# Attention and soft MoE on one core: output tiles of strided tokens, a first head pair loaded ahead, and zero matmuls moved

## The chip, the core and the metric

The kernel runs on one core of one Trainium2 chip. TensorE (PE) multiplies, VectorE (DVE) and ScalarE (ACT) work on tiles, GpSimd (POOL) does a little of that and issues the loads, SyncE (SP) issues the stores. The metric is the device time of one execution in microseconds (us). The kernel before took 154.47 us, the median of three executions (153.16, 154.95 and 154.47).

## What is computed

There are 4 batches, 8 heads, 768 tokens and 64 values per head. Some heads (retrieval heads) see all earlier tokens, the others the first 4 tokens and a window of 64. The attention output of all heads, 3072 tokens of 512 values, is the input x of a soft mixture of 8 experts with 4 slots each.

```python
scores = np.where(mask, q @ k.T / 8, -1e9)      # per batch and head
x = softmax(scores) @ v                          # -> (3072, 512)
logits = x @ phi                                 # phi (512, 32)
d = softmax over tokens of logits                # columns
slot_input = d.T @ x                             # 32 slots
slot_out[e] = np.maximum(slot_input[e] @ w1[e], 0) @ w2[e]
c = softmax over slots of logits                 # rows
out = c @ slot_out                               # (3072, 512) fp32
```

w1 is (8, 512, 1024) and w2 (8, 1024, 512), in fp32.

## The kernel before, in words

The order of all work is written out by hand in one table, ORDER (line 20): Plan.run (line 108) emits one operation after the other, so each engine gets its instructions in that order, and waits for data where it needs them. Names in the table are an operation, a batch or pair, and a part; /A, /D and /P put it on ACT, DVE or POOL.

Loads. All big inputs go through POOL's queue and are cast from fp32 to bf16 on the way. L{q,k,v}{b} (load_qkv, line 250) loads one batch of q, k or v as 96 partitions of 2 x 2048 values, 768 KB written. Partition 24n + t holds token block t of head pair n, so rows 0 to 23 belong to pair 0 (heads 0 and 4). Lw0 to Lw7 are w1 of the eight experts, Lw8 to Lw15 their w2 (load_w, line 263), 1024 KB written each. Twelve buffers (slot) serve raw q, k, v and the weights; Lw12 to Lw15 (lines 656 to 660) go into memory that the attention has freed: parts of qk, vx, xv, and qk again.

Attention. For every batch, T/E (transposes, line 374) transpose the raw rows on PE, 16 transposes and one copy a part, four parts for each of q, k and v. For each of 16 pairs p (4 per batch), QK.p.g makes five groups of scores, EX.p.g their exponentials on ACT, MK.p.g the masks on DVE; V2/VB transpose v, PV.p.i multiplies, NM.p normalises, XT/XE transpose the result into xT.

Experts. For each batch LG makes the logits, EL their exponentials (tile eT, slots along the partitions, tokens along the row), DS and SA sum x over the tokens for each slot. After the last batch SI forms slot_input, H.e.c is the first expert layer (four experts at a time), HR its ReLU, TH/HE a transpose, and W2.e multiplies expert e of 8 into the tile pv; W2.7 is split into a left and a right half. SO.0 and SO.1 scale the halves into slot_out.

Output. EE.b (emit_ee, line 640) copies the exponentials of batch b into expT, so that out_lhs (line 716) is 128 neighbouring columns: an output tile gi (six of them, r = 0 to 3) then holds tokens 512 gi + 4 p + r on partition p. RW (line 721) sums each token's exponentials, OMf multiplies exponentials and slot_out, OEf scales by the inverse sum on ACT or DVE, and STf (line 800) stores: ten stores of 128 partitions, of 1, 2 or 4 rows r each. The stores are SP's only long work, and SP issues them in order.

Zero matmuls. fill (line 324) multiplies tiles of zeros and keeps PE busy. Z0 and Z60 to Z67 stand in the first half, Z1 to Z4 between the steps after the last pair, and Z5 (line 734), eight of them, between W2.6 and W2.7, which is made to wait for it.

Of the kernel before, what the change touches and what calls it, by code (L numbers as in the profile page):

```python
# [20 lines left out]
Lri zero warm Lq0 tables ident Lk0 keypos Tq0.3 flags Tq0.1 Z0 hm0 Eq0.1/A Tq0.2 Eq0.3/D Eq0.2/A Tq0.0 slottab  # L21
Z62 Tk0.3 Eq0.0/D Ek0.3/D ones Tk0.0 Lv0 Z60 Tk0.2 Ek0.0/D Tk0.1 Z61 Ek0.1/D Ek0.2/A QK.0.1 Tv0.1 hm3 Lw0 Lq1
Ev0.1/D EX.0.1 QK.0.0 Tv0.0 EX.0.0 QK.0.3 Ev0.0/D Lk1 EX.0.3 Tv0.2 MK.0.1 Tv0.3 Z66 hm1 Ev0.2/D QK.0.2 Ev0.3/A
Z64 MK.0.3 MK.0.0 V2.0 EX.0.2 QX.0 VB.0/A Z63 V2.3 hm2 QK.0.4 V2.1 VF.0/D VB.3/D MK.0.2 EXX.0 PV.0.0 QK.1.1
EX.0.4 V2.2 Lphi0 PV.0.1 PV.0.2 VB.2/D QK.1.0 PV.0.3 Lv1 EX.1.1 VB.1/D Lw1 Tq1.1 MK.1.1 QK.1.3 EX.1.0 MK.0.4
# [5 lines left out]
MK.3.1 QK.4.4 MK.3.2 Ev1.1/A Lv2 EX.4.4 QK.4.2 Tv1.2 Ev1.2/D MK.3.4 Tv1.0 EX.4.2 PV.3.0 PV.3.1 QK.4.0 Lw3
Tv1.3 PV.3.2 Ev1.0/D QK.4.1 Ev1.3/D PV.3.3 EX.4.0 PV.3.4 V2.4 MK.4.0 Lw4 EX.4.1 QK.4.3 VB.4/D PV.3.5 V2.6
QK.5.0 XT.2 Lw5 EX.4.3 Z65 NM.3 VB.6/A XT.3 XE.2/D EX.5.0 MK.4.1 MK.4.3 XE.3/A QK.5.3 Lq3 Tq2.1 QK.5.1 VF.4/P
MK.5.0 PV.4.0 Eq2.1/D Tq2.0 PV.4.1 EX.5.3 Tq2.2 QX.1 MK.4.2 phi PV.4.2 EX.5.1 EXX.1 PV.4.3 Eq2.2/A MK.5.1
MK.4.4 LG.0 Eq2.0/D QK.5.4 MK.5.3 Tk2.2 Ek2.2/D EL.0 V2.5 EX.5.4 PV.4.4 VB.5/D QK.5.2 TE.0 PV.4.5 Lk3 EX.5.2
MK.5.4 EG.0/D VF.5/P QK.6.0 Tk2.0 NM.4 Ek2.0/D QK.6.1 EX.6.0 MK.5.2 DS.0 QK.6.4 VF.6/P PV.5.0 EX.6.1 PV.5.1
V2.7 SA.0 PV.5.2 QK.6.2 EX.6.4 MK.6.0 PV.5.3 Tv2.1 QK.6.3 PV.5.4 PV.5.5 EX.6.2 MK.6.1 VB.7/D Ev2.1/D XT.4
QK.7.1 Lv3 EX.6.3 MK.6.4 XE.4/A Tk2.1 MK.6.2 QK.7.4 NM.5 MK.6.3 EX.7.1 Tk2.3 PV.6.0 Ek2.1/D PV.6.1 Ek2.3/D
PV.6.2 EX.7.4 QK.7.2 Tq2.3 PV.6.3 QK.7.0 Lw6 EX.7.2 MK.7.1 Eq2.3/D PV.6.4 MK.7.2 PV.6.5 EX.7.0 QK.7.3 Tv2.0
QK.8.2 EX.7.3 NM.6 Ev2.0/D EX.8.2 VF.7/P Tv2.2 Lw7 MK.7.0 QK.8.0 Tv2.3 PV.7.0 PV.7.1 QK.8.1 EX.8.0 Ev2.2/D  # L40
EX.8.1 XT.6 PV.7.2 QX.2 EXX.2 MK.7.3 Ev2.3/D V2.11 XE.6/D MK.7.4 PV.7.3 MK.8.1 VB.11/D QK.8.3 MK.8.2 V2.8
PV.7.4 QK.8.4 PV.7.5 V2.10 EX.8.3 VB.8/D MK.8.0 NM.7 EX.8.4 XT.5 QK.9.1 VF.8/P VB.10/A QK.9.3 EX.9.1 PV.8.0
PV.8.1 PV.8.2 XT.7 XE.5/D MK.8.3 MK.8.4 V2.9 QK.9.2 XE.7/D PV.8.3 PV.8.4 EX.9.3 VB.9/D QK.9.0 PV.8.5 Tq3.0
MK.9.3 VF.10/P MK.9.1 Tq3.2 EX.9.2 QK.10.2 NM.8 EX.9.0 VF.9/P Eq3.2/D LG.1 Tq3.1 EX.10.2 EL.1 Lw8 QK.9.4
Eq3.0/D MK.9.0 Tk3.2 Eq3.1/D MK.9.2 QK.10.0 PV.9.0 EX.9.4 EX.10.0 TE.1 MK.10.2 EG.1/D PV.9.1 PV.9.2 QK.10.1
Tk3.0 MK.9.4 PV.9.3 Ek3.2/D QK.10.3 Ek3.0/D EX.10.1 PV.9.4 PV.9.5 QK.10.4 EX.10.3 MK.10.0 Tk3.3 NM.9 EX.10.4
QK.11.2 Ek3.3/D DS.1 EX.11.2 PV.10.0 QK.11.0 MK.10.1 Tk3.1 PV.10.1 SA.1 EX.11.0 QK.11.1 Tq3.3 VF.11/P Ek3.1/D
# [794 lines left out]
```

## Time and profile before

| | |
|---|---|
| median of three executions | 154.47 us |
| the profiled execution | 154.55 us |
| its span, first to last instruction | 152.7 us |
| mean TensorE clock granted | 0.969 |
| PE, DVE, ACT, POOL busy | 87%, 74%, 70%, 22% of the span |
| bytes read from and written to HBM | 52.50 MB, 6.29 MB |
| loads on POOL's queue | 26.22 MB written, 83.8% of sixteen DMA engines' span |

A span is counted from the first to the last instruction in the profile; the time of the execution holds some 1.8 us more. In the lists of instructions PE is the matmuls and PEld the weight loads; the operand names are the program's tiles, written <- read. An idle time in brackets is that of the engine just before the instruction, with what ended it.

### The profile page before, as it was taken

How to read it: one execution, taken by the hardware profiler on the slowest of the kernel's cores; microseconds unless marked ns; L12 is line 12 of the kernel's file. 1: busy time of each engine (PE TensorE's matmuls, PEld its weight loads, DVE VectorE, ACT ScalarE, POOL GpSimd, SP SyncE). 2: the span in 40 equal slices, each digit the busy share in tenths (PEclk: the TensorE clock that was granted, in tenths of full speed). 3: DMA queues.
4: the chain of work that ended last, by engine and by line, in shares of the span. 5: the costliest groups of instructions: out<-in, count | busy, mean ns of one | idle time of the engine just before them, and what ended most of it. 6: DMA issues, size and time to landing. Idle time of an engine off the chain costs nothing.

```text
span 152.7 us, 5227 instructions
## 1 busy us (share of the span) xinstructions
PE 133.0 (87%) x2313; PEld 83.1 (54%) x2313; DVE 113.4 (74%) x257; ACT 107.5 (70%) x124; POOL 33.5 (22%) x51
## 2 busy tenths in 40 slices
PE   6999799999999999999989999998999689787100
PEld 2355456676677657677656676665673348232000
DVE  3955698999978799999998998999975322166900
ACT  3023699999999999999879999999917710266300
POOL 6910005750031060505520202405110000000000
PEclk9999999999999999999999999999999959999975
DMA  2999999999999999999999999999999992059995
GB/s 34 200 215 224 213 211 211 217 219 225 201 215 213 227 210 212 225 203 216 211 229 215 212 212 223 210 215 219 219 212 215 221 204 58 4 178 411 417 423 219
DMA packets 6950, 32.91 MB, mean 215 GB/s; under 512 B 1296, under 2 KB 1296, under 8 KB 4496
## 3 DMA queue, kind: packets, MB, share of 16 engines
q0 software_dynamic: 4800, 26.22, 83.8%
q1 hardware_dynamic: 2128, 6.37, 10.7%
q8 instruction: 18, 0.29, 0.7%
q14 instruction: 4, 0.03, 0.1%
HBM read 52.50 MB, written 6.29 MB: 385 GB/s over the span
## 4 chain that ended last, share of the span: by engine, by line
PE 59%; DVE 17%; DMA 8%; ACT 5%; issue 3%; POOL 2%; DVEq 0%; POOLq 0%; ACTq 0%
PE pv L522 13%; PE sc L406 13%; PE tr L387 9%; DMA slot<-in_v_dram 8%; DVE pt L418 5%; DVE slot L774 4%; PE sc L330 4%; PE tr L547 4%; PE tr L438 3%; DVE xv L535 3%; PE pv L742 3%; PE sc L561 3%; PE sc L687 3%; ACT pt L474 2%; DVE qk L234 2%
## 5 line engine op out<-in xcount | busy, mean ns | idle before, releaser
L474 ACT ACTIVATE pt<-sc 128x1024 bf16<-128x1024 f32 x80 | 77.6, 1026 | 4.8 <-PE sc L406 3.4
L418 DVE TENSOR_TENSOR pt<-pt,msk 128x512 bf16<-128x512 bf16 (+1 forms) x80 | 37.8, 503 | 1.2 <-ACT pt L474 1.2
L406 PE MATMUL sc<-qk 64*128 64x512 bf16 (+3 forms) x256 | 32.5, 309 | 0.0
L522 PEld LDWEIGHTS <-pt 128*128 128x128 bf16 x640 | 24.7, 97 | 9.1 <-issue 6.4
L522 PE MATMUL pv<-vx,pt 128*128 128x65 bf16 x352 | 27.9, 193 | 0.9 <-DVE xv L535 0.7
L387 PE MATMUL tr<-ident,slot 96*64 96x96 bf16 x768 | 24.1, 209 | 1.7 <-DMA slot<-in_v_dram 0.9
L454 POOL TENSOR_TENSOR vf<-vx,fm 128x528 bf16<-128x528 bf16 x14 | 15.5, 1112 | 44.8 <-DVE vx L234 43.0
L387 PEld LDWEIGHTS <-slot 96*64 96x64 bf16 x768 | 18.9, 110 | 10.6 <-issue 7.7
L522 PE MATMUL pv<-vf,pt 128*128 128x65 bf16 x288 | 22.7, 195 | 0.0
L330 PE MATMUL sc<-zero 128*128 128x512 bf16 x66 | 19.5, 429 | 1.2 <-DVE zero L321 1.2
L234 DVE COPY qk<-tr 128x768 bf16<-128x768 bf16 x28 | 14.9, 550 | 4.7 <-PE tr L387 4.5
L535 DVE TENSOR_TENSOR xv<-pv,rs 128x768 bf16<-128x768 f32 x16 | 15.3, 958 | 0.6
L406 PEld LDWEIGHTS <-qk 64*128 64x128 bf16 x256 | 9.2, 94 | 7.2 <-issue 1.6
L234 DVE COPY xT<-tr 128x768 bf16<-128x768 bf16 (+1 forms) x15 | 8.6, 570 | 5.2 <-PE tr L708 4.2
L239 POOL DMA_DIRECT2D slot<-in_moe_w_dram x12 | 6.8, 569 | 22.7 <-PE tr L387 16.3
L330 PEld LDWEIGHTS <-zero 128*128 128x128 bf16 x66 | 6.2, 108 | 9.1 <-issue 4.4
L232 ACT COPY qk<-tr 128x768 bf16<-128x768 bf16 x4 | 3.2, 797 | 10.8 <-PE tr L387 10.8
L234 DVE COPY xv<-tr 128x768 bf16<-128x768 bf16 x14 | 7.6, 552 | 1.9 <-PE tr L387 1.7
L547 PE MATMUL tr<-ident,xv 128*128 128x128 bf16 x96 | 8.1, 220 | 0.0
L438 PE MATMUL tr<-ident,xv 128*128 128x128 bf16 x96 | 8.0, 220 | 0.0
L234 DVE COPY vx<-tr 128x768 bf16<-128x768 bf16 x12 | 6.4, 551 | 1.0 <-PE tr L438 1.0
L547 PEld LDWEIGHTS <-xv 128*128 128x128 bf16 x96 | 5.6, 97 | 2.1 <-issue 1.8
(102 smaller groups left out, 135.3 us busy)
## 6 DMA issues: line engine op xcount, KB each, us to landing
slot<-in_moe_w_dram POOLq DMA_DIRECT2D x12, 1024.0 KB, 25.5
slot<-in_q_dram POOLq DMA_DIRECT2D x4, 768.0 KB, 18.4
slot<-in_k_dram POOLq DMA_DIRECT2D x4, 768.0 KB, 21.4
slot<-in_v_dram POOLq DMA_DIRECT2D x4, 768.0 KB, 23.7
out_dram<-slot SPq DMA_DIRECT2D x3, 1024.0 KB, 5.6
out_dram<-slot SPq DMA_DIRECT2D x5, 512.0 KB, 3.6
qk<-in_moe_w_dram POOLq DMA_DIRECT2D x2, 1024.0 KB, 18.3
vx<-in_moe_w_dram POOLq DMA_DIRECT2D x1, 1024.0 KB, 21.5
```

The lines of the kernel that those rows point to most:

```text
L234: nc.vector.tensor_copy(dst, src)
L239: emit=lambda o: e.dma_start(dst(), src))
L330: nc.tensor.matmul(scb[buf.slot][:, 0, :], zero[:, 0:128], zero, start=True, stop=True)
L387: nc.tensor.transpose(t[64 * i:64 * (i + 1), :, s, :], rv[:, i, 8 * c + s, :], ident[0:96, 0:96])
L406: nc.tensor.matmul(scb[sc.slot][:, i, c:c + 128 * nb], kk, qq.rearrange("p b c -> p (b c)"), start=True, stop=True)
L418: e.tensor_tensor(pT[:, :, 0:w], pT[:, :, 0:w], mh[:, :, c:c + w], op=ALU.mult)
L438: nc.tensor.transpose(t[:, 128 * j:128 * (j + 1)], vT[:, 6 * n + j, :], ident)
L454: e.tensor_tensor(vfs[VFb[p].slot], vv, mm, op=ALU.mult)
L474: nc.scalar.activation(pTs[PTb[b, n].slot][:, :, 512 * g:512 * (g + 1)], scb[sc.slot], ACT.Exp, scale=scale)
L522: nc.tensor.matmul(pvb[:, h, 65 * i:65 * (i + 1)], lt, rhs, start=(j == 0), stop=(j == i))
L535: nc.vector.tensor_tensor(xo, pvw[:, :, :, 0:64], r.rearrange("p i (j o) -> p i j o", o=1).to_broadcast([P, 2, 6, 64]), op=ALU.mult)
L547: nc.tensor.transpose(t[:, 128 * i:128 * (i + 1)], xv[:, i, 128 * n:128 * (n + 1)], ident)
```

## The change

- Output tiles of strided tokens. EE and expT go. The stationary operand is read straight from eT, in which a token stands 16 columns from the next one used (ef). Tile gi = 0 to 3 holds the tokens of t = gi, x = 0 to 15; gi = 4 and 5 hold x = 16 to 23 for two values of t, one on partitions 0 to 63 and one on 64 to 127, so their matmuls and stores come in two halves. RW has 32 matmuls for 24.
- First head pair first. q and k of batch 0 are loaded in two parts: a, the 24 rows of pair 0, onto partitions 96 to 119, and b, the other 72 rows, onto 0 to 71, in the order q a, k a, q b, k b. Transposes and copies come in parts too (16 operations T where q and k of batch 0 had 8), and QK of pair 0 depends on part a alone.
- Slot tables on GpSimd. The last five instructions of the tables move from DVE to POOL (operation slottab); the first four stay on DVE (slotbits). phi's copy goes from DVE to ACT.
- Zero matmuls. Z5 goes, and with it the dependence of W2.7 on it; Z70 to Z79, two each, are placed by ORDER: four matmuls before W2.7, four between the last steps ahead of W2.0, twelve after the last output matmuls. warm has 13 for 18; Z0 goes.
- ORDER is a new table throughout, of which the diff shows the last lines. Among other moves, the four H now stand as H.1.1, H.1.0, H.0.1, H.0.0, and RW ahead of them.

```diff
-HR.0.1/A H.1.1 HR.0.0/A EE.1/D TH.0 EE.2/A EE.3/D HE.0/D HR.1.1/D H.1.0 RW HR.1.0/A W2.0 W2.1 TH.1 RWR W2.2
-W2.3 HE.1/D W2.4 RC W2.5 W2.6 Z5 W2.7.0 SO.0/A W2.7.1 OMf0L SO.1/D OEf0L OMf0R OMf1 OMf2 OMf3 OEf0R OMf4 OMf5
+LTb LGb.3 ET Z2 EL.3 DS.3 Z3 SA.3 RC SI RW SIE Z4 H.1.1 H.1.0 RWR HR.1.1/D H.0.1 HR.1.0/A H.0.0 TH.1 HR.0.1/A
+Z75 HE.1/D HR.0.0/A TH.0 HE.0/D Z73 W2.0 W2.1 W2.2 W2.3 W2.4 W2.5 W2.6 Z79 Z70 W2.7.0 SO.0/D W2.7.1 OMf0L
...
+    FIRST = {"a": (96, 0, 24), "b": (0, 24, 72)}
...
+    def load_qkv(x, b, part=""):
+        p0, r0, n = raw_parts(x, b)[part]
...
+        lands[x, b, part] = load(f"L{x}{b}{part}", "POOL", n * 2 * 8192, buf, lambda: slots[buf.slot][p0:p0 + n, :]
+                                 .rearrange("p (i x) -> p i x", i=2), src[r0:r0 + n])
...
-    for b in range(B):
-        eto[b] = pl.op(f"EE.{b}", "ACT DVE", deps=[elo[b], dsp] + [xto[p] for p in range(12, 16)],
-                       emit=lambda o, b=b: emit_ee(o, b))
...
-    o_st = pl.op("slottab", "DVE", deps=[o_id, o_kp], emit=emit_slot_tables)
+    o_sb = pl.op("slotbits", "DVE", deps=[o_id, o_kp], emit=emit_slot_bits)
+    o_st = pl.op("slottab", "POOL", deps=[o_sb], emit=emit_slot_tables)
...
+    for i in range(10):
+        fill(f"Z7{i}", 2, [z4])
...
+    ef = eTs.rearrange("p b (k u) -> p u (b k)", u=16)
     def out_lhs(gi, r):
-        return expT[:, r, 128 * gi:128 * (gi + 1)]
+        if gi < 4:
+            return [(slice(0, 128), ef[:, 4 * r + gi, 0:128])]
+        return [(slice(64 * h, 64 * h + 64), ef[:, 4 * r + 2 * (gi - 4) + h, 128:192]) for h in range(2)]
...
+    out_v = out.rearrange("(x t a r) d -> t x a r d", t=4, a=8, r=4)
...
+    def out_dst(gi, r, c):
+        if gi < 4:
+            return [(slice(0, 128), out_v[gi, 0:16, :, r, c])]
+        return [(slice(64 * h, 64 * h + 64), out_v[2 * (gi - 4) + h, 16:24, :, r, c]) for h in range(2)]
...
-            if e == NE - 1 and not z5:
-                z5 = [fill("Z5", 8, w2o[-1:] + [o_rwm])]
...
+        for k, (pr, dst) in enumerate(out_dst(gi, slice(r, r + n), slice(c0, c1))):
+            pl.op(f"ST{'f' if c1 - c0 == 512 else 'r' if c0 else 'l'}{gi}.{r}" + (f".{k}" if gi > 3 else ""), "SP",
+                  deps=[e for x in range(n) for (m, cc), e in oe.items() if m == 4 * gi + r + x and c0 <= cc < c1],
```

The first place is the start of POOL's instructions, which issue the loads. Before (the numbers in slot names are the program's tile numbers, slot_63 being the first buffer, and the shapes are partitions x 2 x 2048):

```order
L239 DMA slot_63<-in_q_dram 96x2x2048
L272 ISA
L272 IOTA xT 128x128
L273 IOTA pc_i 128x1
L274 IOTA xT 128x256
L239 DMA slot_64<-in_k_dram 96x2x2048
L344 MEMSET vx_78 128x48x2
L344 MEMSET vx_79 128x48x2
L239 DMA slot_65<-in_v_dram 96x2x2048
```

Now:

```order
L240 DMA slot_63<-in_q_dram 24x2x2048
L240 DMA slot_64<-in_k_dram 24x2x2048
L287 ISA
L287 IOTA xT 128x128
L288 IOTA pc_i 128x1
L289 IOTA xT 128x256
L240 DMA slot_63<-in_q_dram 72x2x2048
L240 DMA slot_64<-in_k_dram 72x2x2048
L240 DMA slot_65<-in_v_dram 96x2x2048
```

Two loads became four, the two small ones stand ahead of the iotas, and v follows k's second part at once. All later loads follow in the order they had.

The second place is SP's stores, its last instructions. Before:

```order
L802 DMA out_dram<-slot_66 128x512 x2
L802 DMA out_dram<-slot_66 128x1024
L802 DMA out_dram<-slot_70 128x1024 x2
L802 DMA out_dram<-slot_71 128x1024 x2
L802 DMA out_dram<-slot_63 128x2048
L802 DMA out_dram<-slot_64 128x2048
L802 DMA out_dram<-slot_65 128x2048
```

Now:

```order
L844 DMA out_dram<-slot_66 16x8x512 x2
L844 DMA out_dram<-slot_66 16x8x1024
L844 DMA out_dram<-slot_70 16x8x1024 x2
L844 DMA out_dram<-slot_71 16x8x1024 x2
L844 DMA out_dram<-slot_63 16x8x2048
L844 DMA out_dram<-slot_64 8x8x2048 x2
L844 DMA out_dram<-slot_65 8x8x2048 x2
```

The number and the size of the first eight stores are the same, with a target pattern of 16 blocks of 8 where it was 128 rows; the last two became four, of 64 partitions each.

More of the change, by code (lines that the diff above doesn't have):

```diff
@@ L20 @@
 ORDER = """
[L21 to L25, printed above, removed]
@@ L31 @@
[L31 to L35, printed above, removed]
@@ L66 @@
+Z72 Z74 Z77
 """
@@ L400, in sc_mms, with evs @@
+    def evs(x, b, n=None):
+        return [o for part, l in ev[x, b].items() for o in l
+                if n is None or part == "" or (part == "a") == (n == 0)]
     def sc_mms(sc, b, parts):
```

277 lines of the change are left out of this document (153 added, 124 removed).

## The prediction

> **What bounds the kernel now.** I read the slices of the page first, for the transfer engines and the clock.
>
> ```profile
> PEclk9999999999999999999999999999999959999975
> DMA  2999999999999999999999999999999992059995
> GB/s 34 200 215 224 213 211 211 217 219 225 201 215 213 227 210 212 225 203 216 211 229 215 212 212 223 210 215 219 219 212 215 221 204 58 4 178 411 417 423 219
> ```
>
> The sixteen DMA engines are full in 32 slices without a gap, empty in two, and full again to the end. The middle part is the stream of loads: fp32 is read and half as many bytes of bf16 are written, so 215 GB/s counted means some 430 GB/s read. The last part is the stores. The same by stage, in windows:
>
> ```profile
> core 0: us, PE busy (x) PEld busy (x) DVE busy (x) ACT busy (x) POOL busy (x), PEclk, DMA share, GB/s
> 24.00:50.00 26.00, 25.91 (x548) 17.99 (x547) 23.12 (x51) 25.05 (x28) 8.98 (x12) 1.00 1.05 215
> 118.00:125.00 7.00, 5.05 (x79) 2.42 (x72) 2.24 (x4) 3.07 (x4) 0.00 (x0) 0.84 1.01 211
> 125.00:131.40 6.40, 6.40 (x143) 4.50 (x140) 1.23 (x4) 0.39 (x1) 0.00 (x0) 0.91 0.32 67
> 131.40:134.70 3.30, 2.16 (x24) 1.10 (x24) 0.98 (x3) 0.95 (x2) 0.00 (x0) 1.00 0.02 5
> 137.50:149.00 11.50, 3.31 (x11) 0.94 (x10) 6.60 (x10) 3.64 (x6) 0.00 (x0) 0.90 1.02 416
> ```
>
> In the long middle PE (25.91 of 26 us) and ACT (25.05) are as full as the DMA engines, so a view of busy shares cannot say which of the three ends last. The last weights tell. Lw14 (into the tile xv) was issued at 110.2 and Lw15 (into qk, expert 7 of the second layer) at 110.7, and these are their ways to landing:
>
> ```profile
> L239 POOL DMA_DIRECT2D xv<-in_moe_w_dram x1: 592/592/592, 110.2 to 110.2; - x1
> DMA to landing us min/median/max: 13.6/13.6/13.6
> ...
> L239 POOL DMA_DIRECT2D qk<-in_moe_w_dram x1: 536/536/536, 110.7 to 110.7; - x1
> DMA to landing us min/median/max: 17.9/17.9/17.9
> ```
>
> They land at 123.8 and at 110.7 + 17.9 = 128.6 us. Now the timeline at the place where expert 7 is used:
>
> ```profile
> 129.09 0.61 PE L742 MATMUL pv<-xv,xT 128*32 128x256 bf16 x16
> 129.63 1.90 PE L330 MATMUL sc<-zero 128*128 128x512 bf16 x8
> 131.46 0.40 PE L742 MATMUL pv<-qk,xT 128*32 128x256 bf16 x8
> 131.91 0.47 ACT L757 ACTIVATE msk<-pv,rcs 128x256 bf16<-128x256 f32 x1 [6.52 <-PE pv L742]
> 132.44 0.40 PE L742 MATMUL pv<-qk,xT 128*32 128x256 bf16 x8 [0.58 <-ACT msk L757]
> 133.62 0.49 PE L767 MATMUL sc<-msk,xv 128*128 128x256 bf16 x2 [0.56 <-ACT slot L772]
> 134.20 0.48 DVE L774 TENSOR_SCALAR slot<-sc,rrow 128x256 f32<-128x256 f32 x1 [0.76 <-PE sc L767]
> 134.71 11.06 SPq L802 DMA_DIRECT2D out_dram<-slot  x10
> ```
>
> PE ends expert 6 near 129.7, multiplies eight zero tiles (Z5), and starts expert 7 at 131.46. So the loads allow that start only 131.46 - 128.7 = 2.75 us earlier, with 0.1 us for the signal, whatever PE does. From there 134.71 - 131.46 = 3.25 us pass to the first store. The last store and its landing:
>
> ```profile
> L802 SPq DMA_DIRECT2D out_dram<-slot x1: 333/333/333, 145.4 to 145.4; - x1
> DMA to landing us min/median/max: 6.2/6.2/6.2
> ```
>
> It lands at 151.6, 16.9 us after the first was issued; 6.29 MB at 416 GB/s are 15.1 of these. So the kernel's time is: loads to 128.6, what PE adds behind them, 3.25 us, and a store stage that the DMA engines set, then 1.1 us to the end of the span.
>
> **The compute side: gains that the loads swallow.** The chain of waits holds these pieces:
>
> ```profile
> 3.96 12.73 DMA slot<-in_v_dram
> 117.34 1.94 PE sc L687 x32
> 122.76 1.90 PE sc L687 x16
> ```
>
> v lands at 16.7 us, and up to there one exponential has run. With pair 0's q and k rows first, its five exponentials fit ahead of v. Seven took 6.82 us:
>
> ```profile
> 117.20 1.69 DVE L234 COPY xv<-eT 128x768 bf16<-128x768 bf16 x2
> 120.45 1.62 ACT L232 COPY xv<-eT 128x768 bf16<-128x768 bf16 x1
> 99.48 6.82 ACT L474 ACTIVATE pt<-sc 128x1024 bf16<-128x1024 f32 x7
> 122.76 1.90 PE L687 MATMUL sc<-slot,msk 128*32 128x512 bf16 x16 [1.44 <-DVE msk L699]
> 122.75:126.10 3.35, 3.34 (x56) 1.84 (x59) 0.31 (x1) 0.69 (x1) 0.00 (x0) 0.50 0.95 198
> ```
>
> so five are 4.9 us of head start. The first two rows are EE copies, the last two the half-clock matmuls in the timeline, and the windows' row for the stretch (clock 0.50). At the end the four EE copies go (1.6 us each on ACT, 0.85 on DVE), and with the new order H waits no longer for HR.1.1 (1.44 us). Nor must H.1.0 run at half clock: 16 matmuls took 1.90 us, where 32 took 1.94 before. Together 4.9 + 1.44 + 0.95 = 7.3 us: PE would be through with expert 6's predecessors near 122. It then waits for Lw14 (123.8) and for Lw15. Even with half of that gain the loads come last, so all this, and Z5's 1.9 us, is worth 2.75 us in all. The price of the other edits is nothing for the same reason: the slot tables on GpSimd, phi's copy on ACT, 32 column sums (RW) in place of 24, stationary tiles read with a stride, eight more output matmuls, the zero matmuls after the last output. Their cover is the wait for Lw15; if it were gone, they could cost 1 to 2 us together. On POOL, Lv2, Lw3 and Lw4 stand behind the slot tables, which wait for DVE; a load waits long in the queue anyway:
>
> ```profile
> slot<-in_q_dram POOLq DMA_DIRECT2D x4, 768.0 KB, 18.4
> ...
> slot<-in_v_dram POOLq DMA_DIRECT2D x4, 768.0 KB, 23.7
> ```
>
> 786 KB take 3.66 us at 215 GB/s, so some 15 to 20 us of these are queue, and a late issue is hidden.
>
> **The loads.** Bytes and order stay; two loads of 96 partitions become two of 24 and two of 72. The iotas between them (1 us) are covered by the first two, 0.9 us each. What the trace does not show is how sixteen engines share 24 or 72 rows. If evenly, nothing changes. If each such load goes to twelve engines in equal parts, the engines end up unequal: 12 rows each would be even; with the twelve moving on from load to load the fullest get 14, with the same twelve always 16. A row is 3.66 / 6 = 0.61 us of an engine, and every later load waits for the fullest engine, since none of them has a pause to catch up in. So Lw15 lands 0, 1.2 or 2.4 us later. I take 1.2, the middle.
>
> **From Lw15 to the first store.** PE has waited some 3 us for Lw15. Before, the clock was 0.50 from 122.75 to 126.1, after an idle 1.44 us of PE, so I expect a low clock here. The PE pieces of the 3.25 us are two of 0.40 for W2.7 and about 0.2 for each half of the first output tile, 1.2 in all; doubled they add 1.2, at full clock 0. I take 0.8.
>
> **The stores.** Row counts and bytes per partition stay, and so does the 256 KB to 1 MB size of the first eight. The last 2.1 MB (tiles 4 and 5) leave in four stores of 64 partitions, whose target pattern is 8 x 8 x 2048 where it was 128 x 2048. The trace has no such store. At the full 416 GB/s they take 5.0 us, as now. All sixteen engines are full at that rate, 26 GB/s each; if a store of outer count 8 keeps only eight of them, it moves at 208 GB/s, and 2.1 MB take 10.1 us. They are last on a queue that is served in order, so nothing hides the rest: +5.0 us. The upper end, if the new 16 x 8 patterns too ran at half rate and these at a quarter: 4.2 MB at 208 plus 2.1 MB at 104 are 40.3 us in place of 15.1, +25. I take +5.0: half the partitions in one store and an outer count that cannot be cut in sixteen are both steps away from the one shape that the trace shows at full rate.
>
> The Trainium skill, DMA: Bandwidth & Descriptors, in the section Why a DMA increments its semaphore by 16 and not by 1, says that a copy is cut along the slowest dimension of both sides over the largest count up to 16 that divides both. By it the last stores would use 8 engines and the 24- and 72-row loads 12, so its sum is the one taken here; no row of this trace shows it. Without the rule, all sixteen at work on every shape, loads and stores would add nothing (rival 1).
>
> **Sum.** +1.2 (loads) - 2.75 (expert 7 starts at the landing) + 0.8 (clock) + 5.0 (last stores) = +4.25 us. The profiled execution took 154.55 us with a span of 152.7, and the median of three is 154.47, so 158.8 on the one and 158.7 on the other. With both ends of loads and clock: 154.47 + 2.25 = 156.7 to 154.47 + 5.85 = 160.3.
>
> **Rivals.**
> 1. All transfers at the full rate. Then -2.75 + 0.8 = -1.95: 152.5 us, faster by 1.3%. For it: the loads of 96 and of 128 partitions run at the same rate now. Against it: both are multiples of sixteen, and the new shapes aren't. It decides if the last four stores land in under 6 us. Chance 0.13.
> 2. Stores at full rate, loads uneven: -0.75, 153.7 us, no change that shows. A difference of 1% is about what a measurement of this kernel can tell. Chance 0.13.
> 3. Neighbours collide. In the 16 x 8 stores an engine gets eight neighbouring partitions, so that engines may ask for the same part of the memory at the same time, and all stores slow down. Between full and half rate, 4.2 MB at 312 GB/s cost 3.4 us more, and the last 2.1 MB at 156 instead of 208 another 3.4: 165.5 us, and up to 179 at the lower ends. For it: stores now are at the engines' limit, so any collision shows; the loads write bf16 at half that rate and could not show one. Against it: engines that start apart may stay apart. Chance 0.27. The Trainium skill, SBUF — State Buffer, section Door 1: The DMA port swizzle, has four neighbouring partitions on one of sixteen ports and the partitions 32 further on the same; by it engines four apart would meet at one port, at worst all the time.
>
> **How the numbers follow.** The forecast, half the engines for the last four stores, has 0.47, and 158.7 us. The range leaves out rival 1 below 152.4 (some 0.06) and rival 3 above 166 (some 0.13): 152.4 to 166, of which 156.7 to 160.3 is the forecast's own. Faster by over 1% is most of rival 1: 0.12. Within 1% (152.9 to 156.0) is rival 2 and a little of rival 1: 0.16. Slower: 0.72.
>
> **What would show it.** Right: expert 7 starts within 0.2 us of Lw15's landing, PE idle ahead of it, at 129 to 131 us; the GB/s slices fall from some 416 to some 208 for the last 2 MB, with a DMA share near one half; last landing about 22 us after the first store's issue. Loads: Lw15 lands at 128.6 to 131. Wrong: 410 or more to the end (rivals 1 and 2), or a lower rate from the first store on (rival 3). If PE reached expert 7 after Lw15, the view of the loads as the bound would be wrong altogether.

## The result and the profile after

The changed kernel took 166.62 us, the median of four executions (166.05 to 168.75); the kernel before took 154.71 us beside it (153.16 to 156.02). The ratio is 1.079, 95% interval 1.068 to 1.091. The profiled execution of the changed kernel is the slowest of its four (168.75 us), so a stage of it can be up to 2 us longer than usual, and of s_halves below only one of four executions was undisturbed, not the profiled one. These are its places beside those of before, all in us from the start of the span:

| | before | after | difference |
|---|---|---|---|
| last exponential of the attention starts | 109.5 | 117.3 | +7.8 |
| Lw15 (expert 7's weights) landed | 128.6 | 133.4 | +4.8 |
| expert 7 (W2.7.0) starts on PE | 131.46 | 137.54 | +6.1 |
| first store issued | 134.71 | 140.84 | +6.1 |
| from there to the end of the span | 18.0 | 26.1 | +8.1 |
| span | 152.7 | 167.0 | +14.3 |

So the time was lost in two parts: 6.1 us ahead of the first store, 8.1 us behind it. Between the medians the loss is 11.9 us, not 14.3, and the first part is the one that is too large here: s_full, below, does the same work up to its first store and issues it at 138.91, 4.2 us later than before. The slices of the page (one is 4.2 us here) show both:

```profile
PEclk9999555999999999999999999999999999999755
DMA  3999999999999999999999999999997100999551
GB/s 30 174 184 191 218 207 217 217 223 209 212 214 217 224 214 216 206 214 215 223 218 216 214 216 216 214 214 218 220 214 153 41 4 0 290 368 342 214 216 79
```

At the right end the DMA share falls from full to one half, and the rate from 368 to 214 GB/s, where it was 411 to 423 before. At the left end the loads move 174 to 191 GB/s where it was 200 to 224, and three slices have half the clock. Two stages of it in windows, the end of the loads and the stores:

```profile
core 0: us, PE busy (x) PEld busy (x) DVE busy (x) ACT busy (x) POOL busy (x), PEclk, DMA share, GB/s
124.00:126.00 2.00, 1.97 (x30) 1.67 (x30) 0.78 (x4) 0.00 (x0) 0.00 (x0) 1.00 1.01 213
126.00:128.00 2.00, 2.00 (x34) 1.21 (x36) 0.31 (x1) 0.00 (x0) 0.00 (x0) 1.00 0.73 152
128.00:130.00 2.00, 2.00 (x44) 1.02 (x40) 0.75 (x1) 0.28 (x1) 0.00 (x0) 1.00 0.53 111
130.00:132.00 2.00, 1.70 (x23) 0.79 (x16) 0.69 (x1) 1.67 (x3) 0.00 (x0) 1.00 0.29 61
...
145.00:150.00 5.00, 3.00 (x20) 2.05 (x19) 2.25 (x4) 4.57 (x9) 0.00 (x0) 1.00 1.00 364
...
158.00:160.00 2.00, 0.00 (x0) 0.00 (x0) 0.00 (x0) 0.00 (x0) 0.00 (x0) 0.50 0.53 221
160.00:162.00 2.00, 0.00 (x0) 0.00 (x0) 0.00 (x0) 0.00 (x0) 0.00 (x0) 0.50 0.48 205
```

The loads now end in a slope: 0.73, 0.53 and 0.29 of the engines' time over six microseconds. Some engines seem to run out of work long before the others. The stores have two faces: 364 GB/s at a full DMA share (the 16 x 8 stores), then 205 to 221 GB/s at a share of one half (the 64-partition stores). The engines that work at all in these do so at the full rate: 221 GB/s at a share of 0.53 would be 417 at a full one.

The landing of the last weights, and the timeline at expert 7:

```profile
L240 POOL DMA_DIRECT2D qk<-in_moe_w_dram x1: 592/592/592, 116.9 to 116.9; - x1
...
DMA to landing us min/median/max: 16.5/16.5/16.5
```

```profile
131.03 0.59 PE L347 MATMUL sc<-zero 128*128 128x512 bf16 x2
...
132.46 0.59 PE L347 MATMUL sc<-zero 128*128 128x512 bf16 x2
...
133.41 1.93 PE L773 MATMUL pv<-slot,xT 128*32 128x256 bf16 x64 [0.35 <-DVE xT L235]
...
136.58 1.04 PE L347 MATMUL sc<-zero 128*128 128x512 bf16 x4
...
137.54 0.40 PE L773 MATMUL pv<-qk,xT 128*32 128x256 bf16 x8
```

Lw15 lands at 116.9 + 16.5 = 133.4, and expert 7 starts at 137.54: 4.1 us later. No wait for a DMA stands in front of it. PE comes late, and with eight zero matmuls of its own on the way (Z75, Z73, Z79, Z70), as many as Z5 had.

### The profile page after: what moved, and what is told of

It is laid out like the page before. It is cut to its first block, busy times and chain, and to the rows that moved or that the text cites. A ratio compares the mean times of both kernels' runs of the same rounds, so it can differ in the third digit from the quotient of the medians.

```text
span 167.0 us, 5536 instructions
## 1 busy us (share of the span) xinstructions
PE 140.4 (84%) x2456; PEld 89.6 (54%) x2456; DVE 113.8 (68%) x258; ACT 103.6 (62%) x123; POOL 35.4 (21%) x57
## 4 chain that ended last, share of the span: by engine, by line
PE 58%; DVE 17%; DMA 7%; ACT 5%; issue 2%; POOL 2%; ACTq 0%; POOLq 0%; DVEq 0%
PE tr L409 12%; PE pv L549 12%; PE sc L433 12%; DMA slot<-in_k_dram 7%; DVE pt L445 7%; PE sc L347 6%; ACT slot L805 3%; PE tr L574 3%; DVE xv L562 3%; PE tr L465 3%; PE sc L588 2%; PE pv L773 2%; PE sc L709 2%; DVE vx L235 2%; DVE slot L807 2%
## 5 line engine op out<-in xcount | busy, mean ns | idle before, releaser
L501 ACT ACTIVATE pt<-sc 128x1024 bf16<-128x1024 f32 x80 | 78.5, 1024 | 12.0 <-PE sc L433 10.0
L445 DVE TENSOR_TENSOR pt<-pt,msk 128x512 bf16<-128x512 bf16 (+1 forms) x80 | 38.7, 516 | 0.0
L433 PE MATMUL sc<-qk 64*128 64x256 bf16 (+3 forms) x256 | 33.5, 317 | 1.3 <-issue 1.3
L409 PE MATMUL tr<-ident,slot 96*64 96x96 bf16 (+2 forms) x896 | 28.5, 212 | 1.2 <-DMA slot<-in_k_dram 0.5
L409 PEld LDWEIGHTS <-slot 96*64 96x64 bf16 (+2 forms) x896 | 22.6, 117 | 12.7 <-issue 10.1
L347 PE MATMUL sc<-zero 128*128 128x512 bf16 x65 | 21.2, 458 | 3.7 <-DVE slot L807 2.5
L235 DVE COPY qk<-tr 128x768 bf16<-128x768 bf16 (+2 forms) x35 | 16.3, 476 | 7.6 <-PE tr L409 7.4
L235 DVE COPY xv<-tr 128x768 bf16<-128x768 bf16 x16 | 8.8, 554 | 2.4 <-PE tr L409 2.2
L235 DVE COPY vx<-tr 128x768 bf16<-128x768 bf16 x16 | 8.7, 551 | 2.2 <-PE tr L465 2.1
L465 PEld LDWEIGHTS <-xv 128*128 128x128 bf16 x96 | 6.2, 103 | 2.0 <-issue 1.6
L574 PEld LDWEIGHTS <-xv 128*128 128x128 bf16 x96 | 5.5, 97 | 2.3 <-issue 2.0
(99 smaller groups left out, 128.6 us busy)
```

What stands on the lines that cost most here:

```text
L235: nc.vector.tensor_copy(dst, src)
L347: nc.tensor.matmul(scb[buf.slot][:, 0, :], zero[:, 0:128], zero, start=True, stop=True)
L409: nc.tensor.transpose(t[64 * i:64 * (i + 1), :, s, :], rv[:, i, 8 * c + s, :], ident[p0:p0 + n, p0:p0 + n])
L433: nc.tensor.matmul(scb[sc.slot][:, i, c:c + 128 * nb], kk, qq.rearrange("p b c -> p (b c)"), start=True, stop=True)
L445: e.tensor_tensor(pT[:, :, 0:w], pT[:, :, 0:w], mh[:, :, c:c + w], op=ALU.mult)
L465: nc.tensor.transpose(t[:, 128 * j:128 * (j + 1)], vT[:, 6 * n + j, :], ident)
```

## The experiments

Theory after the result: (1) the targets of the stores cost about 8 us, half the engines for the last four and a smaller loss in the 16 x 8 ones; (2) the half clock from 16 to 30 us put PE behind. Rivals: for (1), tiles that come late from ACT and DVE, or scattered rows; for (2), the loads of 24 and 72 rows, or the new order itself.

### The stores: targets taken back, all, in part, and scattered

s_full stores all tiles as before:

```diff
+    oc = out.rearrange("(g p r) d -> g p r d", p=128, r=4)
     def out_dst(gi, r, c):
+        if True:
+            return [(slice(0, 128), oc[gi, :, r, c])]
```

> The changed kernel with all six output tiles stored in the target pattern of the kernel before (128 partitions to 512 neighbouring rows; the tokens land in other rows than they should, nothing else is changed). In the changed kernel 24.8 us pass from the first store's issue (140.84) to the last store packet (165.65), in the one before 16.6 (134.71 to 151.28). Theory (the targets make the stores slow): 16.6 to 17.5 us, 410 GB/s or more to the end, and a median of 166.6 - 7.5 = 159 us. Rival (the tiles come late from ACT and DVE, which take 10 us for them): still 22 us or more, and 164 us or more.

Measured: 159.07 us (158.79 to 159.74), ratio to before 1.031 (1.027 to 1.036), and 157.2 - 138.91 = 18.3 us from the first store to the end of the span. Its store stage in windows:

```profile
143.00:145.00 2.00, 2.00 (x14) 1.41 (x13) 1.21 (x2) 2.00 (x5) 0.00 (x0) 1.00 1.01 414
145.00:150.00 5.00, 2.29 (x14) 1.24 (x12) 2.37 (x4) 3.09 (x6) 0.00 (x0) 1.00 1.03 424
150.00:154.00 4.00, 1.53 (x8) 0.48 (x5) 0.00 (x0) 0.00 (x0) 0.00 (x0) 1.00 1.02 426
```

414 to 426 GB/s from 143 us on. The targets make the whole 7.8 us (26.1 - 18.3; 7.6 between the medians); ACT and DVE, which do the same work here, make none.

s_halves takes back tiles 0 to 3 alone (`if gi < 4`), s_16x8 tiles 4 and 5 alone (`if gi > 3`).

> The changed kernel with tiles 0 to 3 stored in the target pattern of the kernel before (tokens of these in other rows) and the four 64-partition stores of tiles 4 and 5 as the change has them. Theory (half the engines for outer count 8): the last 2.1 MB still move at 200 to 220 GB/s, 10 us, the 4.2 MB ahead of them at 415 in place of 366 to 377; 22.5 us from first issue to last packet, 164.5 us. Rival (neighbouring partitions collide and that is what slows the last stores as well): the last four stores at more than 300 GB/s once the others are out of their way, 160 us.

> The changed kernel with tiles 4 and 5 stored whole in the target pattern of the kernel before (tokens of these in other rows), tiles 0 to 3 in the 16 x 8 pattern as the change has them. In the changed kernel the eight 16 x 8 stores took 15.0 us from the first issue to the last landing (140.84 to 155.87), with the pattern of before 12.3 (138.91 to 151.25). Theory (two separate costs): 15 us for these eight again, then 4.9 us for tiles 4 and 5 in place of 9.8, and a median of 166.3 - 5 = 161.5 us. Rival (an engine only makes up later what the first stores leave; the two costs are one): tiles 4 and 5 at under 350 GB/s as well, 163 us or more.

s_halves: 164.17 us in the one execution that counts (164.5 expected), without an interval. Its windows show the two kinds of store apart:

```profile
148.00:150.00 2.00, 0.00 (x0) 0.00 (x0) 0.47 (x1) 2.00 (x4) 0.00 (x0) 1.00 1.05 426
...
158.00:160.00 2.00, 0.00 (x0) 0.00 (x0) 0.00 (x0) 0.00 (x0) 0.00 (x0) 0.50 0.51 205
160.00:162.00 2.00, 0.00 (x0) 0.00 (x0) 0.00 (x0) 0.00 (x0) 0.00 (x0) 0.50 0.51 213
```

426 GB/s for the tiles in the old pattern, 205 to 213 at half the share for the 64-partition stores, with nothing else in their way: these have half of the engines, and do not speed up when left alone. Half the partitions do not by themselves mean half the engines: l_even's first loads, of 32 and 64 partitions, have a full share (its page, 4 to 12 us). So the outer count of 8 is the reading that fits, but no store of 64 partitions with another outer count was run. One thing in this trace is not explained: from 152 to 158 us the same stores moved only 106 to 180 GB/s at a share of 0.49, and the whole stage took 25.9 us to the end of the span, 0.2 less than in the changed kernel.

s_16x8: 163.64 us (162.52 to 164.64), ratio 1.062 (1.054 to 1.069), 161.3 - 138.94 = 22.4 us from the first store to the end:

```profile
138.90:141.00 2.10, 1.31 (x7) 0.73 (x6) 1.98 (x4) 1.18 (x3) 0.00 (x0) 1.00 0.36 82
141.00:145.00 4.00, 2.51 (x16) 1.68 (x15) 2.34 (x4) 3.46 (x7) 0.00 (x0) 1.00 1.02 327
145.00:150.00 5.00, 2.24 (x13) 1.24 (x12) 2.39 (x4) 3.12 (x6) 0.00 (x0) 1.00 1.05 383
...
155.00:160.00 5.00, 0.00 (x0) 0.00 (x0) 0.00 (x0) 0.00 (x0) 0.00 (x0) 0.50 0.61 256
```

The 16 x 8 pattern alone costs 22.4 - 18.3 = 4.1 us, more than the theory's 2.7: it starts slowly (82 GB/s in the first 2.1 us, where s_full moved 216), moves 327 and 383 where s_full moved 382 to 424, and falls to 311 from 150 to 152 us. At its end the share goes down in a slope (0.74, 0.22 and 0.08 from 157 to 160 us) where s_full's falls from 0.99 to 0.05 at once, so it seems to leave engines with unequal rests; the 256 GB/s above are a mean over that end. Of the two signs of the rival, that the two costs are partly one, the time came (over 163 us) and the rate did not: tiles 4 and 5 went at 377 to 434 GB/s from 154 to 157 us, not under 350. The halves cost only 26.1 - 22.4 = 3.7 us on top. Together they are 7.8; how the sum splits stays open. By the times, 16 x 8 is worth from 2.4 us (166.62 - 164.17) to the 4.1, and the halves from 3.7 to 5.1 (164.17 - 159.07).

s_stride scatters the rows, but keeps an outer count of 128:

```diff
+    oc = out.rearrange("(p g r) d -> g p r d", g=6, r=4)
     def out_dst(gi, r, c):
+        return [(slice(0, 128), oc[gi, :, r, c])]
```

> The changed kernel with all six tiles stored whole, partition p of tile gi to the four rows from 24 p + 4 gi on (tokens in other rows): the target is as scattered as in the change, 8 KB pieces far apart, but its outer count is 128. Theory (it is the 16 x 8 cut, not the scattering, that slows the eight first stores): 12.3 us from first issue to last landing of the first eight, 16.8 us in all, 159 us as with the pattern of before. Rival (pieces that lie apart in HBM are slower): 15 us for the first eight, 19.5 us in all, 161.5 us or more.

Measured: 160.89 us (159.55 to 161.88), and 160.1 - 141.81 = 18.3 us from the first store to the end, to the tenth that of s_full:

```profile
145.00:150.00 5.00, 3.24 (x20) 2.21 (x20) 2.20 (x4) 4.57 (x9) 0.00 (x0) 1.00 1.02 406
150.00:155.00 5.00, 2.75 (x12) 1.06 (x11) 1.41 (x2) 1.43 (x3) 0.00 (x0) 1.00 1.04 427
```

Scattered rows cost nothing; the cut 16 x 8 does. (The time is longer than s_full's ahead of the first store, where this execution had half the clock longest; more on that below.) That neighbouring partitions collide is the reading that fits, but no run shows the collision itself.

### What made PE late: clock or loads

c_fill adds zero matmuls in the front, l_even splits q and k of batch 0 differently:

```diff
-hm1 Tq0b.1 ... EX.0.3 QK.0.4 Eq0b.2/D EX.0.1 EX.0.4 Eq0b.0/D Tk0b.1
+hm1 Tq0b.1 ... EX.0.3 Z80 QK.0.4 Eq0b.2/D EX.0.1 EX.0.4 Eq0b.0/D Z81 Tk0b.1
```

```diff
-    FIRST = {"a": (96, 0, 24), "b": (0, 24, 72)}
+    FIRST = {"a": (96, 0, 32), "b": (0, 32, 64)}
```

> The changed kernel with eleven more zero matmuls on PE at 14 to 18 us, six ahead of QK.0.4 and five ahead of Tk0b.1, where PE has 2 us of idle time. Theory (half clock puts PE behind): the clock is 1.00 from 16 to 30 us, EX number 20 starts near 41 us (46.8 in the changed kernel, 40.1 in the one before), expert 7 starts at the landing of Lw15 near 133.5 in place of 137.5, and the time is 162.5 us. Rival (the loads, 3.6 us late from v on, put PE behind): the clock is full, but EX number 20 starts no earlier than 45 and the time is 165.5 us or more.

> The changed kernel with q and k of batch 0 split in 32 and 64 rows in place of 24 and 72 (pair 0 still depends on the first part alone). Lv0 landed at 20.2 us in place of 16.7, Lw15 at 133.4 in place of 128.6. Theory (24 and 72 rows use twelve engines): v lands at 17 us, Lw15 below 130. If the half clock from 16.2 to 29.9 us is what put PE behind, and it stays, W2.7 still starts at 136 to 138 and the time is 165 to 167 us; if the late loads are what put PE behind, W2.7 starts 3.6 us earlier and the time is 162.5 us.

c_fill: 167.24 us (166.05 to 168.08), ratio 1.081 (1.075 to 1.088): nothing gained. In its windows the half clock lasts 6.8 us in place of 13.7:

```profile
11.40:18.20 6.80, 6.80 (x80) 3.29 (x79) 4.47 (x17) 3.07 (x3) 0.55 (x1) 0.50 1.13 193
18.20:30.00 11.80, 11.74 (x213) 6.73 (x211) 8.13 (x21) 8.65 (x11) 0.00 (x0) 1.00 1.04 211
```

The exponentials' line, cut off at the 21st (count, ns of one, first and last start), hardly moved. For the changed kernel and then for c_fill:

```profile
L501 ACT ACTIVATE pt<-sc x21: 1017/1024/1030, 12.1 to 46.8; 128x1024 bf16<-128x1024 f32 x21
```

```profile
L511 ACT ACTIVATE pt<-sc x21: 1018/1023/1030, 13.0 to 45.8; 128x1024 bf16<-128x1024 f32 x21
```

45.8 in place of 46.8, where the theory said 41. My theory of the clock falls as the main cause. Yet the clock is not free, and five traces say what it costs. s_full, s_16x8, s_halves and s_stride do the same work as the changed kernel up to the stores, and v lands between 19.8 and 20.7 us in all of them. The half clock ends at 24.1 us in s_16x8, at 24.4 in s_full, at 29.2 in s_halves, at 29.9 in the changed kernel and at 31.2 in s_stride; in the same order the 21st exponential starts at 44.8, 44.9, 46.4, 46.8 and 47.8. Here are s_full and s_stride:

```profile
L501 ACT ACTIVATE pt<-sc x21: 1017/1024/1029, 11.9 to 44.9; 128x1024 bf16<-128x1024 f32 x21
```

```profile
L501 ACT ACTIVATE pt<-sc x21: 1017/1024/1030, 11.7 to 47.8; 128x1024 bf16<-128x1024 f32 x21
```

A half clock that ends 5 to 7 us later, well past the landing of v, goes with a delay of 1.5 to 3 us, which reaches the first store (138.91 in s_full, 141.81 in s_stride). The 1.9 us by which the changed kernel's profile is behind s_full are of this kind. But none of the five starts it before 44.8, and l_even, below, does. c_fill had half the clock for no longer than s_16x8 (6.8 us) and was later by 1.0; its eleven zero matmuls take time on PE too.

l_even: 164.42 us (164.16 to 165.25), ratio 1.066 (1.061 to 1.072). The same line, and then the landing of v:

```profile
L501 ACT ACTIVATE pt<-sc x21: 1017/1024/1029, 12.1 to 41.5; 128x1024 bf16<-128x1024 f32 x21
```

```profile
L240 POOL DMA_DIRECT2D slot<-in_v_dram x1: 679/679/679, 4.7 to 4.7; - x1
...
DMA to landing us min/median/max: 11.8/11.8/11.8
```

v lands at 4.7 + 11.8 = 16.5 in place of 20.2, Lw15 at 111.6 + 18.1 = 129.7 in place of 133.4, the 21st exponential starts 5.3 us earlier (3.4 earlier than in s_full), the last one too (112.0), and the loads end sharply again (windows of l_even):

```profile
124.00:126.00 2.00, 2.00 (x32) 0.86 (x28) 0.75 (x1) 0.18 (x1) 0.00 (x0) 0.66 1.02 213
126.00:128.00 2.00, 2.00 (x30) 0.87 (x18) 0.39 (x1) 1.53 (x3) 0.00 (x0) 1.00 0.49 102
128.00:130.00 2.00, 1.35 (x19) 0.86 (x22) 0.99 (x2) 0.24 (x1) 0.00 (x0) 1.00 0.08 16
```

So the row counts make the loads late, and the late loads make the attention late. W2.7 starts at 133.93, 3.6 us earlier, as I had written for late loads. The median of 164.42 lies between the two times that I had written down: 1.9 of the 5.3 us are the clock of the changed kernel's profile, as above, and H now met a half clock, with 5.32 us for its 64 matmuls (from 121.6 to 126.9) in place of 3.64.

b_uneven does that part alone, in the kernel before:

```diff
+        cut = [(0, 24), (24, 96)] if b == 0 and x != "v" else [(0, 96)]
```

> The kernel before with q and k of batch 0 loaded as 24 and 72 rows, in its own order, pair 0 waiting for both parts as it did. Theory (the row counts alone make the loads late, and what comes late into the front is not made up): v lands at 20 us in place of 16.7, Lw15 at 132 in place of 128.6, exponential 20 at 43 in place of 40.1, and the time is 157.5 us. Rival (only the new order suffers from it, the old one has the zero matmuls Z5 and the wait for Lw15 as a reserve): Lw15 late by the same, but the time at 155.5 us or less.

Measured: 157.32 us (157.12 to 157.54), ratio 1.018 (1.013 to 1.024), Lw15 at 113.3 + 18.2 = 131.5, and

```profile
L476 ACT ACTIVATE pt<-sc x21: 1018/1023/1045, 18.8 to 42.6; 128x1024 bf16<-128x1024 f32 x21
```

2.5 us later than the 40.1 of before. All as expected but v (18.4): 24 and 72 rows cost 2 to 3 us in both orders, and what comes late at the front is not made up in 130 us.

### Both repairs, and what is left

e_full has the edits of s_full and l_even; e_nozero leaves out Z65, Z60 and Z67 besides.

> The changed kernel with both repairs at once: q and k of batch 0 in 32 and 64 rows, and all stores in the target pattern of the kernel before (tokens in other rows). Theory (the two costs lie one behind the other and add): first store at 137 us, 16.8 us of stores, a median of 164.4 - 7.4 = 157 us, still 2.5 us above the kernel before. Rival (with the stores out of the way the earlier start of the exponentials shows): 154 us or less.

> The kernel with both repairs (32 and 64 rows, stores as before) without nine zero matmuls in the attention: Z65, Z60 and Z67, at 22.4, 33.1 and 39.4 us when the loads are even. Theory (PE's own work, not the exponentials, sets the pace of the attention, so that neither the head start on ACT nor anything else off PE counts): the nine, 0.21 us each, come off one for one; exponential number 40 starts 1.5 to 1.9 us earlier than at 65.0 and the last stores too, a median of 155.3 us. Rival (ACT sets the pace, 80 exponentials of 1 us each and what stands between them): number 40 within 0.4 us of 65.0, and 156.7 us or more.

e_full: 157.74 us (156.17 to 158.06), ratio 1.021 (1.013 to 1.029): the two costs add, and 2 to 3 us remain. e_nozero: 156.94 us (154.74 to 158.82), ratio 1.015 (1.010 to 1.019). It is inconclusive: in the profiled execution (158.82 us) PE had half the clock for 13.7 us of the front, and exponential 40 came at 66.3, later than with the zeros. The pace had to be tested by adding work. A first edit for that (e_pe) left the program as e_full has it; e_pe2 has it right:

```diff
-                for j in range(6):
+                for j in range(12 if b in (1, 2) else 6):
+                    j %= 6
```

> The kernel with both repairs, with the eight transposes V2.4 to V2.11 done twice each on PE (same output): 48 more transposes, 3 to 4 us of PE time between 45 and 95 us, no more work on any other engine. Theory (PE sets the pace there): exponential 60 starts 2.5 to 3.5 us later than the 88.8 us with both repairs, and the time grows to 160.5 us. Rival (ACT sets the pace): exponential 60 within 0.7 us of 88.8, and the time within 1 us of 157.7.

> The kernel with both repairs, with the eight transposes V2.4 to V2.11 really done twice each (48 transposes more on PE, same output; the earlier edit left the program as it was). Theory (PE sets the pace of the attention): the 48 take 48 x 0.07 = 3.4 us of PE at least, exponential 60 starts 2.5 us or more later than 88.2 to 88.8, and the time is 159.5 us or more. Rival (PE is full only because it waits inside its own pipeline; ACT or DVE set the pace): exponential 60 within 1 us of 88.5, and the time within 1 us of 157.2.

e_pe is a second look at e_full: 156.65 us (155.91 to 158.12). It and e_pe2 both had the full clock up to the stores. The group of V2's transposes (count, us busy) in e_pe and in e_pe2:

```profile
L466 PE MATMUL tr<-ident,xv 128*128 128x128 bf16 x96 | 7.9, 220 | 0.3 <-DVE slot_acc L657 0.3
```

```profile
L466 PE MATMUL tr<-ident,xv 128*128 128x128 bf16 x144 | 10.6, 220 | 0.3 <-DVE slot_acc L657 0.3
```

Here are the exponentials up to the 61st, in the same order:

```profile
L502 ACT ACTIVATE pt<-sc x61: 1015/1023/1047, 12.7 to 88.2; 128x1024 bf16<-128x1024 f32 x61
```

```profile
L502 ACT ACTIVATE pt<-sc x61: 1015/1023/1043, 12.5 to 90.5; 128x1024 bf16<-128x1024 f32 x61
```

2.7 us more of PE delay the exponentials by 2.3, a little less than the 2.5 that I had written, and the first store by 2.3 (135.41 to 137.71). PE sets the pace there, between some 45 and 90 us, though ACT was as good as full too (25.05 of 26 us in the kernel before). The median moved less than I wrote (158.22, 156.78 to 159.0); the executions of either program differ among themselves by 2 us.

e_pe also shows what the two repairs leave where no half clock comes in: its first store at 135.41 is 0.7 us later than that of the kernel before. In e_full the same program had half the clock near 17 us and again near 122 us, and its first store came at 137.68.

e_vfd moves the last four products from POOL to DVE (three of them, VF.12, VF.14 and VF.15, stood on POOL in the kernel before too); e_vfd_fill adds ten zero matmuls in the front to it (Z80, Z81 and Z82):

```diff
-VF.12/P ... VF.13/P ... VF.14/P ... VF.15/P
+VF.12/D ... VF.13/D ... VF.14/D ... VF.15/D
```

> The kernel with both repairs, with VF.12 to VF.15 on DVE in place of POOL. With both repairs the last five pairs took 23.7 us from exponential 60 to 79, in the kernel before 20.2; DVE is full there (4.97 of 5 us at 100 to 105), and masks beside a product on POOL took up to 1.81 us in place of 0.41. Theory (these masks are what the new order loses by): no mask over 0.6 us there, 3.9 us of DVE time saved for 2.8 spent, exponentials 60 to 79 in 22.5 us, and 156.5 us. Rival (the masks wait on something else, and DVE only gets more work): 24 us or more there, and 158 us or more.

> The kernel with both repairs and VF.12 to VF.15 on DVE, with ten more zero matmuls on PE between 14 and 20 us. The same program came out with 3.4 us of half clock near 16.5 us and again near 122 us (first store at 137.7), and with none (135.4). Theory (what is left of the loss is the clock, and PE's idle time ahead of v decides it): clock full from 6 to 120 us, first store at 134.5 to 135.5, 153.5 to 154.5 us, as the kernel before. Rival (the clock is lost elsewhere or costs nothing): 155.5 us or more, as without the ten.

The timeline of e_full has the masks (line 445, DVE) beside the products (line 481, POOL):

```profile
96.65 2.27 POOL L481 TENSOR_TENSOR vf<-vx,fm 128x528 bf16<-128x528 bf16 x2 [0.95 <-DVE vx L235]
96.88 3.46 DVE L445 TENSOR_TENSOR pt<-pt,msk 128x512 bf16<-128x512 bf16 x5
...
104.97 0.41 DVE L445 TENSOR_TENSOR pt<-pt,msk 128x512 bf16<-128x512 bf16 x1
...
108.57 2.15 DVE L445 TENSOR_TENSOR pt<-pt,msk 128x512 bf16<-128x512 bf16 x2
109.01 1.08 POOL L481 TENSOR_TENSOR vf<-vx,fm 128x528 bf16<-128x528 bf16 x1
```

A mask of 128x512 takes 0.41 us alone; two beside one product take 2.15, five beside two 3.46. With the products on DVE:

```profile
97.01 1.42 DVE L445 TENSOR_TENSOR pt<-pt,msk 128x512 bf16<-128x512 bf16 x4
98.35 0.70 DVE L481 TENSOR_TENSOR vf<-vx,fm 128x528 bf16<-128x528 bf16 x1
```

e_vfd: 155.54 us (153.54 to 156.7), ratio 1.002 (0.996 to 1.007); the last exponential starts at 110.9 in place of 112.5. No mask there takes more than 0.55 us, and exponentials 60 to 79 take 22.0 us in place of 23.7, as the theory had it. The longest mask in e_full, 1.81 us in place of 0.41 beside products of some 1.1 us, agrees with the Trainium skill, SBUF — State Buffer, section Who interferes with whom, where DVE and GpSimd lock each other out of a shared pair of ports for a whole instruction.

e_vfd_fill: 156.80 us (155.84 to 157.71), ratio 1.020 (1.016 to 1.024). In the windows of e_vfd, and then of e_vfd_fill, the one has half the clock in its front and the other has none:

```profile
15.30:22.10 6.80, 6.80 (x82) 3.14 (x76) 3.51 (x11) 4.04 (x6) 0.00 (x0) 0.50 1.01 210
```

```profile
16.00:22.00 6.00, 5.84 (x135) 3.50 (x136) 4.15 (x12) 4.38 (x7) 0.00 (x0) 1.00 1.02 211
118.50:121.90 3.40, 3.15 (x52) 2.72 (x57) 0.75 (x3) 0.00 (x0) 0.00 (x0) 0.99 1.03 214
121.90:125.30 3.40, 3.40 (x36) 1.33 (x32) 0.75 (x1) 0.54 (x1) 0.00 (x0) 0.50 1.03 214
```

Still the 21st exponential starts at 42.1 in both. Ten zero matmuls are work for PE too, so this shows that nothing is gained by buying the clock back with them here, not that half a clock is free. Both runs have half the clock near 122 us, where H runs: 5.32 us for its 64 matmuls in e_vfd, 3.64 in the changed kernel's profile at full clock. These 1.7 us are most of the 2.0 that separate e_vfd's first store (136.67) from that of before (134.71). That e_vfd's fastest executions are those without it is argued, not shown: the three of 153.54 to 154.0 us have mean clocks of 0.989 and 0.990, the other seven 0.957 to 0.977, but none of the three was profiled.

### The zero matmuls at the end, alone

```diff
-W2.6 Z5 W2.7.0
+W2.6 W2.7.0
```

> The kernel before without the eight zero matmuls Z5 ahead of expert 7, which then needs Lw15 alone (no other part of the change). Theory (as predicted for this part): PE ends expert 6 at 129.65 and starts expert 7 there, 1.8 us earlier than before, since Lw15 has landed at 128.6; clock full, so the first store is 1.8 us earlier and the median 152.7 us, 1.2% under the kernel before. Rival (the zeros keep the clock up and pay for themselves): PE at half clock for the output tiles, 154 to 155.5 us.

Measured over 12 executions: 153.32 us (152.67 to 154.23), ratio 0.996 (0.993 to 0.999). The timeline:

```profile
127.79 0.61 PE L740 MATMUL pv<-xv,xT 128*32 128x256 bf16 x16
129.73 0.40 PE L740 MATMUL pv<-qk,xT 128*32 128x256 bf16 x8 [1.32 <-DMA qk<-in_moe_w_dram]
```

Expert 7 waits 1.32 us for Lw15 and starts as it lands (110.7 + 19.0 = 129.7). The mechanism is the forecast's. In the profiled executions the gain is 1.3 us (154.55 to 153.21), the first store comes 1.5 us earlier (133.24) in place of 1.8, and the first output matmuls met half the clock from 132.0 to 135.4 us. Between the medians it is only 0.3 us or 0.4%, not 1.2%, as most executions of the kernel before beside it took less than the profiled one (median 153.62); why the medians differ less than the traces stays open. It is the one version here whose interval lies below the kernel before, and by less than the 1% that the forecast called measurable. With Lw15 at 129, 3.3 us to the first store, 18 to the end of the span and 1.8 around it, some 152 us are my estimate of the floor of this way to load and store.

## Why the prediction was wrong, step by step

The direction was right, 158.7 us was 7.9 too low, and 166.62 lies 0.6 above the range. The sum was +4.25; it came out at +14.3 in the profiled executions and at +11.9 between the medians:

- **Ahead of the first store: -0.75 forecast, +6.1 measured, +4.2 in s_full.** This is the step that failed: "The compute side: gains that the loads swallow". The loads did not come last: PE reached expert 7 4.1 us after Lw15 had landed, the sign by which the forecast called its own view wrong altogether. Of s_full's 4.2 us, 3.5 go with even loads (e_pe's first store at 135.41, where neither had half the clock between the attention and the stores), and 0.7 stay in place of the gain. I took five exponentials done early for 4.9 us of head start, because ACT was as full as PE. The exponentials did start early (first at 12.1 in place of 15.9). With even loads the sixth was still 3.3 us ahead (20.9 against 24.2), and by the 21st nothing was left (41.5 against 40.1). The 61st is 0.5 to 1.1 us ahead again (88.8 in e_full, 88.2 in e_pe, 89.3 before), and the last 2.4 to 3.0 behind. e_pe2 shows why a head start on ACT counts for little: between some 45 and 90 us PE sets the pace, and such a head start takes no work off PE. That this holds ahead of 45 us too, where the head start went, is argued from there; what the new order does on PE in that stretch was not taken apart.
- **Loads: +1.2 forecast, at most 2.4.** That 24 and 72 rows make the loads late was right (l_even takes it away), and the slope at the end of the loads fits engines unequally loaded. The size was 3.5 us at v and 4.8 at Lw15; even rows take off 3.7 at both. That is more than unequal shares were to give at most; part of it is a lower rate while the engines are busy (174 to 191 GB/s in the first slices), and why is open. Above all the delay was charged to the wrong end: I added it to Lw15's landing, while the late start reached PE's own work, which came last.
- **"The price of the other edits is nothing".** The new order has four products on POOL beside masks on a full DVE; moving them away gains 1.6 us (112.5 to 110.9 in e_vfd). The kernel before had three of the four there too, but its masks of that stage took 1.23 us at most, against 1.81. With the four, exponentials 60 to 79 took 23.7 us, without them 22.0, in the kernel before 20.2; what makes the other 1.8 is open. The cover of these edits, the wait for Lw15, did not exist, as PE came after Lw15.
- **Z5 and the tail.** From the last exponential to expert 7 it was 22.0 us and is 20.2, a gain of 1.8 where I had counted Z5's 1.9, the wait of 1.44 and 0.95 of clock. Eight zero matmuls stand in it, as many as Z5 had, and the forecast did not count them. The -2.75 presumed that Lw15 would end the wait; b_noz5 shows that true in the old order.
- **From Lw15 to the first store: +0.8 for half the clock.** From the start of expert 7 it was 3.30 us in place of 3.25: nothing. PE did not wait for Lw15, so the idle time that was to lower the clock did not come.
- **Stores: +5.0 forecast, +8.1 measured.** The last four stores did go at 205 to 221 GB/s and half the DMA share, as the sign said. What was missing is rival 3's first part: the 16 x 8 stores at 311 to 383 GB/s in place of 382 to 426, 2.4 to 4.1 us. Rival 3 had that loss on top of the half rate, and a second one, the last stores at 156 GB/s, which the changed kernel does not show. By its price, 165.5 us, rival 3 came nearest, but by luck: the second loss, which did not come, stood in for the time ahead of the first store, for which it had no place.

The Trainium skill, DMA: Bandwidth & Descriptors, section Why a DMA increments its semaphore by 16 and not by 1, on which one sentence of the forecast drew, agrees with s_halves (half the share) and, in the direction, with l_even against the change, though the 3.7 us between these two are more than the 2.4 worked out at most.

## What to carry to other kernels

Before a transfer gets a new shape, count what the cut over the engines makes of its outer dimension: 128 partitions to 128 pieces ran at 406 to 427 GB/s even with scattered rows, 16 x 8 at 311 to 383, 8 x 8 at half the DMA share and mostly 200 to 221, and loads of 24 and 72 rows made the later ones some 3 us late. Where PE, ACT and the DMA engines are all as good as full, busy shares don't say which one sets the pace; double a little work on one of them and see whether the end moves by as much. Before a profile's stages are compared, look at the clock of both executions: here 1.9 us of one stage were the clock of one execution. An edit costed at nothing because a wait covers it needs that wait to exist in the new kernel too.

## What the runs showed of the hardware

- What makes the first loads late makes the last load late too, a hundred microseconds on: Lw15 landed at 133.4 with 24 and 72 rows and at 129.7 with 32 and 64, in the old order at 131.5 with 24 and 72 and at 128.6 with 96. That single engines stay behind is the reading that fits the slope at the end; no view shows single engines.
- The rate of a store falls at a full DMA share (364 in the changed kernel, 424 in s_full, both from 145 to 150 us), so the share alone doesn't tell a healthy transfer.
- The clock was halved behind windows in which PE was far from idle (3.15 of 3.40 us busy at 118.5 to 121.9 in e_vfd_fill, most of it 32 matmuls of one column each), and the same program got it in one execution (e_full) and not in another (e_pe).
- The same work up to the stores, with the loads landing alike, had its 21st exponential at 44.8 to 44.9 us where the half clock ended by 24.4 and at 47.8 where it lasted to 31.2.
- A mask of 0.41 us on DVE took up to 1.81 us when a product ran on POOL.
